# An attention, expert and feed-forward kernel: its first sixteen attention groups and first sixteen product pieces in one written order of stages, with another order of loads

## The chip, the cores and the metric

The kernel runs on one core of a Trainium2 chip. A core has five engines that run side by side, each through its own queue in program order: TensorE (PE; PEld is its weight load), VectorE (DVE), ScalarE (ACT), GpSimd (POOL) and SyncE (SP), which here only issues transfers. They wait for one another through semaphores. The metric is device time in microseconds (us) of one execution, the median of several runs; less is better.

## The reference

Three layers follow one another, all in float32: a masked attention, a dense mixture of 8 experts with a gate that is balanced by eight rounds of row and column scaling, and a feed-forward layer. Cut to what matters:

```python
# q, k, v: (4 batches, 8 heads, 576, 64); heads 0-3 local, heads 4-7 strided
scores = scale * np.matmul(q, k.transpose(0, 1, 3, 2))
mask_local = (rel >= 0) & (rel < 32)
mask_strided = (rel >= 0) & (pos[None, :] % 32 == pos[:, None] % 32)
...
attn = softmax(np.where(masks, scores, -1e9))
x = np.matmul(attn, v)             # becomes 2304 tokens x 512
...
P = balanced(np.exp(x @ w_gate))   # 2304 x 8
for e in range(8):
    out += P[:, e:e + 1] * (np.maximum(x @ w1[e], 0.0) @ w2[e])   # 512 -> 1024 -> 512
...
h = out @ w_in                     # 512 -> 2048
result = (h * sigmoid(1.702 * h)) @ w_out
```

## The kernel before

**Products.** Every float32 matrix product is done with each factor split into a high and a low part of a type that TensorE takes in one pass (fp32r): high by an ACT copy, low by a subtraction on DVE or POOL, and three of the four part products are summed. For weights this is `split_into` (ACT L270, POOL or DVE L264), for inputs `split_input` (ACT L576, DVE or POOL L581). Experts are worked off in units of 256 hidden columns over a block of 768 tokens. Work on units is cut into **pieces**, numbered in one list from 0 on: a product of six matmuls (L1048), or a "down" piece, the second product of one tile of 128 tokens (L1314 to L1316, six matmuls). `advance()` issues the next piece and with it the tasks in `side[number]` (splits, sums, loads). The first two units are done plainly, in halves of 384 tokens (`half_product`): pieces 0 to 3 are four products of unit 0, from piece 4 on products and downs alternate. Each second product of a column is followed by `activate`: high part on ACT (hh, L1085), low part on DVE (hl, L1088); a down piece needs the hh and hl of the half before it.

**Attention.** There are 32 attention groups. A local group (two tiles of 96 queries, two heads) goes through score matmuls S (PE L770), mask M (DVE L785), row maximum L (DVE L795), exponential E (ACT L802, four), reciprocal of the sums D (DVE L814, L815), scaling N (POOL L816), transposition T (PE L827), copy out C (ACT or DVE), value product V (PE L851) and copy K into the block of tokens (DVE L863). A strided, "compact" group has the same stages with other instructions (S is L665, C is four ACT copies L723, T runs on DVE). X below is `split_input` of a quarter of the block, W and Y are `split_plain` and `split_w2`, splits of the first two units' weights.

**What sets the order.** A step i issues N and D of group i-2, V and K of group i-4, T and C of i-3, E of i-1, then S, M and L of group i: lockstep, one new group each step. Between the stages stand gaps. In steps 0 to 9 a gap gives idle matmuls that read only zeros (`keep_warm`, L1461), 1.5 on average; in steps 10 to 15 it gives 0.6 pieces and otherwise an idle matmul; from step 16 on it gives 1.5 pieces:

```python
for i in range(NSTEP):
    if i == NHALF + 4:
        quota[0] = 0.0
    att_step(i, fill_first if i < NHALF + 4 else fill_half if i < NFIRST + 4 else fill)
    for t in ahead.pop(i, ()):
        t()
```

`ahead` holds, by step, the weight loads and the splits W, Y and X. Before the first step the loads are issued on SP's queue: the two first local pairs, their values, two compact pairs, their values. When the last step is over, pieces go on until piece 105 is done; then the gate and all else follow in a fixed order.

Of the kernel before, what the change touches and what calls it, by code (L numbers as in the profile page):

```python
# [8 lines left out]
F32 = mybir.dt.float32  # L9
# [3 lines left out]
ALU = mybir.AluOpType  # L13
# [18 lines left out]
IDLE_FIRST = 6  # L32
IDLE_GAP = 1.5


RATE_HALF = 0.6
# [21 lines left out]
def strided_attention_moe_ffn(  # L58
# [643 lines left out]
    def compact_normalise(i, b, pair):  # L702
        _, s, st = att[b, pair, -1]
        den = st[:, 1, :]
        nc.vector.tensor_reduce(out=den, in_=s, axis=AX.X, op=ALU.add)
        nc.vector.tensor_scalar_add(den, den, EPS)
        nc.vector.reciprocal(out=den, in_=den)
        nc.gpsimd.tensor_tensor(
            out=s, in0=s, in1=den[:, :, None].to_broadcast([P, 2 * CQ, CLEN]), op=ALU.mult
        )  # L710

    def compact_transpose(i, b, pair):
        e, _, _ = att[b, pair, -1]
        eT = ap.tile([P, 4, P], F32, tag="eT", name="eT")
        nc.vector.transpose(eT.rearrange("p n q -> p (n q)"), e)
        src = eT.rearrange("p n (m q) -> p (n m) q", q=Q)
        for c in range(CG):
            rows = slice(c * Q, c * Q + CLEN)
            o = wide[rows, :, c * CLEN : (c + 1) * CLEN]
            if c % 2 and i >= NFIRST:  # L720
                nc.gpsimd.tensor_copy(o, src[rows, :, :CLEN])
            else:
                nc.scalar.activation(out=o, in_=src[rows, :, :CLEN], func=AF.Copy)  # L723

    def compact_values(i, b, pair):
# [3 lines left out]
        for h in range(2):  # L729
            if i < NALONE:  # L730
                av = ps.tile([P, 512], F32, tag="AB"[h], name="av")
            elif h:
                av = down_bank("av") if i >= NFIRST else ps.tile([P, 512], F32, tag="B", name="av")
            else:
                av = eps.tile([P, 512], F32, tag="pa", name="av")
# [74 lines left out]
    def att_normalise(i, b, pair, g):  # L810
        s, st, U, R, C = att[b, pair, g]
        n = 2 * U
        den = st[:R, 1, :n]
        nc.vector.tensor_scalar_add(den, den, EPS)  # L814
        nc.vector.reciprocal(out=den, in_=den)  # L815
        nc.gpsimd.tensor_tensor(  # L816
            out=s, in0=s, in1=den[:, :, None].to_broadcast([R, n, C]), op=ALU.mult
        )

    def att_transpose(i, b, pair, g):  # L820
        s, _, U, R, C = att[b, pair, g]
        if i < NALONE:
            pt = ps.tile([P, 4, P], F32, tag="AB"[i % 2], name="pt")
        else:
            pt = eps.tile([P, 4, P], F32, tag="pa", name="pt")
# [14 lines left out]
    def att_values(i, b, pair, g):  # L840
        eT, U, R, C = att.pop((b, pair, g))
        vt = att_in["v", b, pair]
        if i < NALONE - 1 and i % 2:
            av = ps.tile([P, 512], F32, tag="C", name="av")
        elif NALONE - 1 <= i < NFIRST:
            av = ps.tile([P, 512], F32, tag="B", name="av")
        else:
            av = down_bank("av")
# [36 lines left out]
    NALONE = NHALF + 1  # L885
    STAGES = [
        (2, att_normalise, False),
        (4, att_values, True),
        (3, att_transpose, True),
        (1, att_exp, False),  # L890
        (0, att_scores, True),
    ]
# [14 lines left out]
    def att_step(i, fill):  # L907
# [11 lines left out]
        def loads():  # L919
            for p in LOAD_QK[i]:  # L920
                load_qk(*p, q=nc.scalar)
            for p in LOAD_V[i]:
                load_v(*p, q=nc.scalar)

        if i < NHALF + 4:
            for d, stage, gap in STAGES:
                for t in run(d, stage):
                    t()
                if gap:
                    fill()  # L930
        else:
            run(2, att_normalise)
            first, apart = run(4, att_values), 4 <= i < n + 4 and groups[i - 4][2] < 0
            if apart:
                for t in first:
                    t()
                first = ()
                fill()
            second, third = run(3, att_transpose), run(0, att_scores)
            for t in first + second:  # L940
                t()
            if not apart:
                fill()
            for t in third[:1]:
                t()
            run(1, att_exp)
            loads()
            fill()
            for t in third[1:]:
                t()  # L950
            fill()
        if i < NHALF + 4:
            loads()

# [498 lines left out]
    with tc.manual_schedule():  # L1453
# [39 lines left out]

        quota = [0.0]
        ahead = defaultdict(list)
        QUARTERS = ("W11", "W21", "W12", "W22")
        ahead[1].append(lambda: load_w1(0))
        ahead[3].append(lambda: load_w2(0))
        ahead[4].append(lambda: load_w1(1))
        for m, pair in enumerate(PAIRS[:2]):  # L1500
            ahead[5 + m].append(lambda pair=pair: load_vc(1, pair))
        for n, what in enumerate(QUARTERS):
            ahead[(4, 5, 7, 8)[n]].append(lambda what=what: split_plain(0, what))
            ahead[9 + n].append(lambda what=what: split_plain(1, what))
        for ft in range(2):
            ahead[7 + ft].append(lambda ft=ft: split_w2(0, ft))
            ahead[12 + ft].append(lambda ft=ft: split_w2(1, ft))
        ahead[10].append(lambda: load_w1(2))
        ahead[9].append(lambda: load_w2(1))

        ahead[NHALF + 2].append(lambda: split_input(0))
        ahead[NHALF + 3].append(lambda: split_input(3))
        ahead[14].append(lambda: split_input(6))
        ahead[NFIRST + 3].append(lambda: split_input("X21"))
        BY_HALF = 4 * PLAIN + 3 * (PLAIN - 1)

        def fill_first():
            quota[0] += IDLE_GAP
            keep_warm(int(quota[0]))
            quota[0] -= int(quota[0])  # L1520

        def fill_half():
            quota[0] += RATE_HALF
            if quota[0] >= 1 and done[0] < BY_HALF:
                advance()
                quota[0] -= 1
            else:
                keep_warm(1)
# [7 lines left out]
        plan_first_sums()  # L1536
        side[20].append(lambda: gate_logits(0))
        for i in range(NSTEP):
            if i == NHALF + 4:
                quota[0] = 0.0  # L1540
            att_step(i, fill_first if i < NHALF + 4 else fill_half if i < NFIRST + 4 else fill)
            for t in ahead.pop(i, ()):
                t()
# [115 lines left out]
```

## Time and profile before

| | us |
|---|---|
| median of 3 runs (1958.81 to 1960.32) | 1959.04 |
| the profiled execution, its own time | 1957.69 |
| its span, first to last instruction | 1955.9 |
| PE busy in the span | 1917.5 (98%) |
| DVE busy | 1455.9 (74%) |
| ACT busy | 853.1 (44%) |
| POOL busy | 1244.9 (64%) |

A time is read against the engines: where PE is busy all the time, only less work for PE helps; where it isn't, the order of the work and its waits set the time. PE's busy time counts idle matmuls too. In rows, "us" after a start is a duration; "[1.2 <-DVE e L785]" says that the engine stood idle for 1.2 us before, until that instruction of DVE was done.

### The profile page before, as it was taken

How to read it: one execution, taken by the hardware profiler on the slowest of the kernel's cores; microseconds unless marked ns; L12 is line 12 of the kernel's file. 1: busy time of each engine (PE TensorE's matmuls, PEld its weight loads, DVE VectorE, ACT ScalarE, POOL GpSimd, SP SyncE). 2: the span in 40 equal slices, each digit the busy share in tenths (PEclk: the TensorE clock that was granted, in tenths of full speed). 3: DMA queues.
4: the chain of work that ended last, by engine and by line, in shares of the span. 5: the costliest groups of instructions: out<-in, count | busy, mean ns of one | idle time of the engine just before them, and what ended most of it. 6: DMA issues, size and time to landing. Idle time of an engine off the chain costs nothing.

```text
span 1955.9 us, 35146 instructions
## 1 busy us (share of the span) xinstructions
PE 1917.5 (98%) x11716; PEld 1792.3 (92%) x11716; DVE 1455.9 (74%) x2715; ACT 853.1 (44%) x2079; POOL 1244.9 (64%) x1282
## 2 busy tenths in 40 slices
PE   7999999999999999999999999999999999999999
PEld 5778778888888999999999999999999998888888
DVE  5788677777677788788878788888886766756555
ACT  4555456666765433333333433333333445533332
POOL 3456566777777677777767888888887767600100
PEclk8999999999999999999999999999999999999999
DMA  6468789999997998988898789999999867665663
GB/s 219 149 217 289 263 283 325 368 344 354 367 330 246 317 311 288 299 288 287 282 297 288 252 302 313 333 321 323 358 312 325 288 220 266 233 193 186 218 196 122
DMA packets 284451, 546.18 MB, mean 279 GB/s; under 512 B 30864, under 2 KB 52720, under 8 KB 283376
## 3 DMA queue, kind: packets, MB, share of 16 engines
q1 hardware_dynamic: 280816, 532.08, 79.4%
q10 hardware_dynamic: 3456, 11.87, 2.0%
q8 instruction: 94, 1.54, 0.3%
q14 instruction: 85, 0.70, 0.1%
HBM read 382.30 MB, written 161.53 MB: 278 GB/s over the span
## 4 chain that ended last, share of the span: by engine, by line
PE 62%; DVE 2%; DMA 2%; POOL 2%; issue 1%; ACT 0%; SPq 0%; ACTq 0%; DVEq 0%; POOLq 0%
PE y L1209 21%; PE pA L1048 17%; PE pC L1048 9%; PE pB L1048 4%; PE y L1316 4%; PE y L1315 4%; PE y L1314 4%; DMA w<-s1moe 1%; POOL s L1181 1%; DMA w<-s7moe 1%; POOL comb L1156 1%; DMA rows<-prd 0%; DVE xs L565 0%; DMA ws<-fw 0%; DVE r L1162 0%
## 5 line engine op out<-in xcount | busy, mean ns | idle before, releaser
L1048 PE MATMUL pA<-xc,w 128*128 128x384 f32 x2880 | 573.4, 336 | 2.7 <-DVE pB L1104 2.2
L1209 PE MATMUL y<-comb,w 128*128 128x384 f32 x2688 | 537.8, 334 | 2.2 <-DVE sum L1219 1.0
L1048 PEld LDWEIGHTS pA<-xc,w 128*128 128x128 f32 x2880 | 508.9, 188 | 19.8 <-DVE pB L1104 3.6
L1209 PEld LDWEIGHTS y<-comb,w 128*128 128x128 f32 x2688 | 472.0, 188 | 3.5 <-DVE sum L1219 1.7
L1156 POOL TENSOR_TENSOR comb<-s,comb 128x384 fp32r<-128x384 f32 x256 | 283.5, 1118 | 91.4 <-ACT comb L1151 82.3
L1219 DVE TENSOR_TENSOR sum<-y,sum 128x384 f32<-128x384 f32 x420 | 231.4, 552 | 100.2 <-PE y L1209 97.7
L1048 PE MATMUL pC<-xc,w 128*128 128x384 f32 x1464 | 295.8, 336 | 0.0
L1316 PE MATMUL y<-w,hl 128*128 128x512 f32 x672 | 268.3, 399 | 5.0 <-DVE hl L1088 4.6
L1314 PE MATMUL y<-w,hh 128*128 128x512 f32 x672 | 264.3, 393 | 6.8 <-DVE acc L1329 2.8
L1048 PEld LDWEIGHTS pC<-xc,w 128*128 128x128 f32 x1464 | 259.8, 188 | 9.8
L1315 PE MATMUL y<-w,hh 128*128 128x512 f32 x672 | 265.6, 395 | 0.0
L1151 ACT ACTIVATE comb<-r 128x384 fp32r<-128x384 f32 x192 | 101.3, 528 | 363.1 <-DVE r L1162 350.0
L1316 PEld LDWEIGHTS y<-w,hl 128*128 128x128 f32 x672 | 126.2, 188 | 36.0 <-DVE hl L1088 8.8
L1314 PEld LDWEIGHTS y<-w,hh 128*128 128x128 f32 x672 | 126.4, 188 | 27.0 <-DVE acc L1329 3.4
L264 POOL TENSOR_TENSOR w<-raw,w 128x512 fp32r<-128x512 f32 (+1 forms) x104 | 120.8, 1176 | 35.7 <-ACT w L270 35.4
L1048 PE MATMUL pB<-xc,w 128*128 128x384 f32 x708 | 142.2, 335 | 0.0
L1315 PEld LDWEIGHTS y<-w,hh 128*128 128x128 f32 x672 | 126.2, 188 | 15.8
L1156 POOL TENSOR_TENSOR comb<-r,comb 128x384 fp32r<-128x384 f32 x64 | 67.8, 1060 | 112.7 <-ACT comb L1151 112.7
L270 ACT ACTIVATE w<-raw 128x256 fp32r<-128x256 f32 (+1 forms) x307 | 135.6, 461 | 8.9 <-POOL raw L234 8.8
L1151 ACT ACTIVATE comb<-s 128x384 fp32r<-128x384 f32 x256 | 131.8, 515 | 11.0 <-POOL s L1181 10.9
L1181 POOL TENSOR_TENSOR s<-r,r 128x384 f32<-128x384 f32 x127 | 134.2, 1077 | 2.1 <-DVE r L1162 2.0
L1343 DVE TENSOR_TENSOR acc<-y,acc 128x512 f32<-128x512 f32 x126 | 86.8, 689 | 62.7 <-PE y L1316 62.6
(178 smaller groups left out, 2827.2 us busy)
## 6 DMA issues: line engine op xcount, KB each, us to landing
w<-s1moe SPq DMA_DIRECT2D x448, 256.0 KB, 4.9
w<-s7moe SPq DMA_DIRECT2D x448, 256.0 KB, 4.9
s1moe<-w SPq DMA_DIRECT2D x216, 256.0 KB, 5.0
w<-s1ffn SPq DMA_DIRECT2D x133, 256.0 KB, 2.8
s7moe<-kw SPq DMA_DIRECT2D x116, 256.0 KB, 4.9
s7moe<-w SPq DMA_DIRECT2D x96, 256.0 KB, 4.8
w<-s2ffn SPq DMA_DIRECT2D x38, 512.0 KB, 3.7
raw<-wa SPq DMA_DIRECT2D x32, 512.0 KB, 5.9
```

Of the source, the lines that this page charges most:

```text
L264: eng.tensor_tensor(out=t[:, 1], in0=src, in1=f(high), op=ALU.subtract)
L270: nc.scalar.activation(out=high, in_=src, func=AF.Copy)
L1048: nc.tensor.matmul(out=o, lhsT=w[:, hw, kk * P : (kk + 1) * P], rhs=x[:, hx, kk, :], start=opens and m == 0, stop=ends and m == len(todo) - 1,
L1151: nc.scalar.activation(out=t[:, 0, :], in_=part[i, q], func=AF.Copy)
L1156: eng.tensor_tensor(out=t[:, 1, :], in0=part[i, q], in1=f(t[:, 0, :]), op=ALU.subtract)
L1181: eng.tensor_tensor(out=part[i, q], in0=part[i, a], in1=part[i, b], op=op)
L1209: nc.tensor.matmul(out=o, lhsT=t[:, hw, dt * P : (dt + 1) * P], rhs=x[:, hx, :], start=(n == 0), stop=(n == 5))
L1219: nc.vector.tensor_tensor(out=a, in0=o, in1=a, op=ALU.add)
L1314: nc.tensor.matmul(out=o, lhsT=hh[:, c], rhs=w[:, 0], start=(m == 0), stop=False)
L1315: nc.tensor.matmul(out=o, lhsT=hh[:, c], rhs=w[:, 1], start=False, stop=False)
L1316: nc.tensor.matmul(out=o, lhsT=hl[:, c], rhs=w[:, 0], start=False, stop=(m == 1))
L1343: nc.vector.tensor_tensor(out=a, in0=y, in1=a, op=ALU.add)
```

## The change

The sixteen first steps are replaced by a list of tokens, START, worked off in order. A letter is a stage and the number its group: S scores, M mask, L maximum, E exponential, D sums and reciprocal, N scaling, T transposition, C its copy, V values, K copy into the block. `:p`, `:A`, `:B`, `:C` name the PSUM bank. i3 is three idle matmuls, W, Y and X are the splits, q and v loads of a pair, A2 and B1 weight loads, P the next piece. So stages that went together (M and L with S, N with D, C with T, K with V) are issued apart. After START the steps 16 to 35 run as before, and the same piece, 105, is reached where they end. START holds pieces 0 to 15; sixteen steps held 0 to 9.

```diff
+START = (
+    "S0 M0 i2 S1 L0 M1 E0 L1 i2 S2 E1 D0 N0 M2 q12 L2 i3 T0:p D1 S4 E2 N1 C0 M4 V0:B L4 T1:p D2 S3 E4 M3 "
+    "N2 C1 L3 i3 V1:C D4 E3 T2 N4 K1 i2 S8 K0 C2 T4:p D3 M8 N3 i1 S6 L8 C4 T3:A M6 E8 V4:B C3 V3:C K4 D8 "
+    "W210 S5 W110 K3 W120 L6 X0 V2:BC E6 K2 P0 q13 N8 D6 M5 N6 T8:p L5 S7 C8 E5 V8:B D5 T6:p q10 M7 N5 C6 "
+    "K8 L7 W121 i1 V6:B W221 T5 E7 S9 v10 D7 v11 C5 K6 N7 M9 Y00 T7 i3 V5:BC W111 L9 W220 S10 q11 Y01 K5 "
+    "E9 M10 X3 i2 S12 W211 A2 C7 D9 i1 P1 B1 L10 N9 V7:pB M12 E10 T9 P2 K7 C9 P3 D10 L12 N10 S11 P4 E12 "
+    "M11 L11 P5 Y11 Y10 V9:pB E11 K9 P6 D11 T10:p D12 N11 X6 P7 N12 C10 T11:p S13 V10:B q22 C11 P8 K10 "
+    "M13 V11:B K11 P9 XX21 T12:p S14 P10 L13 C12 P11 E13 M14 P12 S15 q20 D13 i1 P13 L14 N13 M15 E14 L15 "
+    "P14 i3 P15 "
+).split()
...
         nc.scalar.dma_start(out=cst, in_=consts)
+        load_qk(0, PAIRS[0])
         for p in EARLY:
             load_qk(*p, rest)
             load_v(*p)
-        for pair in PAIRS[:2]:
-            load_qk(0, pair)
-        for pair in PAIRS[:2]:
-            load_vc(0, pair)
+        load_vc(0, PAIRS[0])
+        load_qk(0, PAIRS[1])
+        load_vc(0, PAIRS[1])
         nc.gpsimd.memset(wide, 0.0)
         nc.vector.memset(wgr, 0.0)
+        load_w1(0)
         nc.sync.dma_start(out=wgr[:, :, :E], in_=wg)
+        load_w2(0)
+        load_w1(1)
+        for pair in PAIRS[:2]:
+            load_vc(1, pair)
...
+        for token in START:
+            key, _, banks = token.partition(":")
+            if key[0] == "i":
+                keep_warm(int(key[1:]))
+            elif key[0] == "P":
+                advance()
+            else:
+                ops[key](tuple(BANK[x] for x in banks))
         quota = [0.0]
```

SP's queue, the first loads, before (a row is one transfer or several alike; qkt are queries and keys, vt and vc values; qkt_133 is the first compact pair):

```order
L638 DMA qkt_116<-qk 128x2x192 x2
L638 DMA qkt_116<-qk 128x2x384
L648 DMA vt_128<-vw 128x768
L638 DMA qkt_116<-qk 128x2x384
L648 DMA vt_131<-vw 128x768
L641 DMA qkt_133<-qk 128x1152
L641 DMA qkt_135<-qk 128x1152
L655 DMA vc_137<-vc 128x1024
L655 DMA vc_139<-vc 128x1024
L1478 DMA wgr_88<-wg 128x4x8
L217 DMA raw1_175<-wa 128x1024
```

and of the change, where the first compact pair is qkt_127:

```order
L646 DMA qkt_116<-qk 128x2x192 x2
L649 DMA qkt_127<-qk 128x1152
L646 DMA qkt_116<-qk 128x2x384
L656 DMA vt_130<-vw 128x768
L646 DMA qkt_116<-qk 128x2x384
L656 DMA vt_133<-vw 128x768
L663 DMA vc_135<-vc 128x1024
L649 DMA qkt_137<-qk 128x1152
L663 DMA vc_139<-vc 128x1024
L225 DMA raw1_143<-wa 128x1024
L1498 DMA wgr_88<-wg 128x4x8
```

That pair's load moves ahead of four transfers, and the first weight load (raw1) stands behind the compact values as before, now ahead of the gate's.

PE's queue around the first piece (pA is its output, xc the split input, w1 a split weight, sc scores, av values, pt a transposition), before:

```order
L827 MATMUL pt_660<-cst_87,e_470 128x96 x4
L1461 MATMUL idle_out_115<-idle_113 128x384
L665 MATMUL sc_672<-qkt_575 32x18 x64
L1461 MATMUL idle_out_115<-idle_113 128x384 x2
L851 MATMUL av_759<-eT_665,vt_128 64x96 x4
L770 MATMUL sc_770<-qkt_613 96x128 x4
L1461 MATMUL idle_out_115<-idle_113 128x384
L1048 MATMUL pA_781<-xc_625,w1_323 128x384 x6
L1461 MATMUL idle_out_115<-idle_113 128x384
L739 MATMUL av_800<-wide_110,vc_425 64x72 x8
L739 MATMUL av_809<-wide_110,vc_425 64x72 x8
L1048 MATMUL pA_781<-xc_624,w1_427 128x384 x6
```

and of the change:

```order
L857 MATMUL av_376<-eT_350,vt_133 64x96 x4
L857 MATMUL av_382<-eT_370,vt_130 64x96 x4
L673 MATMUL sc_394<-qkt_137 32x18 x64
L752 MATMUL av_481<-wide_110,vc_135 64x72 x8
L752 MATMUL av_490<-wide_110,vc_135 64x72 x8
L1067 MATMUL pA_505<-xc_472,w1_462 128x384 x6
L838 MATMUL pt_520<-cst_87,e_338 128x96 x4
L673 MATMUL sc_528<-qkt_257 32x18 x64
L857 MATMUL av_598<-eT_525,vt_133 64x96 x4
L838 MATMUL pt_606<-cst_87,e_361 128x96 x4
L1480 MATMUL idle_out_115<-idle_113 128x384
L857 MATMUL av_625<-eT_611,vt_130 64x96 x4
```

The first product stands between the values of the first compact group and a transposition, more than twenty rows earlier on PE, with one idle matmul near it in place of five.

ACT's queue around the first two high parts (hh11 and hh12), before:

```order
L723 ACTIVATE wide_110<-eT_764 18x16x18 x4
L700 ACTIVATE e_737<-e_737 128x16x18
L270 ACTIVATE w1_790<-raw1_321 128x256
L1085 ACTIVATE hh11_828<-pA_781 128x384
L802 ACTIVATE e_775,st_776<-e_775,st_776 96x128 x4
L648 DMA vt_851<-vw 128x768
L270 ACTIVATE w1_862<-raw1_321 128x256
L723 ACTIVATE wide_110<-eT_873 18x16x18 x4
L1085 ACTIVATE hh12_893<-pC_855 128x384
```

and of the change:

```order
L708 ACTIVATE e_702<-e_702 128x16x18
L584 ACTIVATE xc_471<-x_103 128x768
L278 ACTIVATE w1_786<-raw1_148 128x256
L736 ACTIVATE wide_110<-eT_724 18x16x18 x4
L1104 ACTIVATE hh11_806<-pA_505 128x384
L815 ACTIVATE e_762,st_763<-e_762,st_763 96x128 x4
L736 ACTIVATE wide_110<-eT_837 18x16x18 x4
L1104 ACTIVATE hh12_860<-pC_839 128x384
```

Before, the four copies into `wide` stood straight ahead of the second high part alone, and a weight split ahead of the first; now they stand straight ahead of both, and the next exponentials (e) behind.

## Rows read from the trace of the kernel before

**Rows 1.** Busy time of each engine in four stretches of the span

```profile
core 0: us, PE busy (x) PEld busy (x) DVE busy (x) ACT busy (x) POOL busy (x), PEclk, DMA share, GB/s
0.00:78.83 78.83, 63.12 (x955) 49.77 (x956) 46.08 (x111) 38.56 (x132) 27.22 (x35) 0.85 0.60 199
78.83:100.00 21.17, 20.87 (x280) 17.36 (x281) 15.78 (x32) 10.28 (x32) 13.48 (x15) 1.00 0.38 124
100.00:200.00 100.00, 96.48 (x1054) 80.35 (x1053) 81.51 (x175) 54.91 (x179) 60.03 (x72) 1.00 0.76 261
200.00:300.00 100.00, 92.81 (x519) 78.94 (x519) 71.78 (x163) 50.58 (x139) 64.81 (x81) 0.98 0.79 272
```

**Rows 2.** By line, first 78.83 us: count, busy us, mean ns, idle before

```profile
L1461 PE MATMUL idle_out<-idle 128*128 128x384 f32 x59 | 22.6, 472 | 1.3 <-DVE idle L1456 1.3
L802 ACT ACTIVATE e<-e,st 96x128 f32<-96x128 f32 x44 | 17.2, 392 | 8.2 <-DVE st L795 8.1
...
L785 DVE SCALAR_TENSOR_TENSOR e<-sc,msk 96x512 f32<-96x512 f32 x12 | 8.2, 682 | 8.4 <-PE sc L770 8.1
...
L581 DVE TENSOR_TENSOR xc<-x,xc 128x768 fp32r<-128x768 f32 x3 | 3.5, 1155 | 2.4 <-ACT xc L576 2.4
...
L814 DVE TENSOR_SCALAR st<-st 96x4 f32<-96x4 f32 x10 | 2.9, 287 | 1.2 <-ACT e L802 1.2
...
L1327 DVE COPY acc<-y 128x512 f32<-128x512 f32 x3 | 2.1, 692 | 2.6 <-PE y L1316 2.6
...
L1088 DVE SCALAR_TENSOR_TENSOR hl<-pA,hh 128x384 fp32r<-128x384 f32 x2 | 1.1, 553 | 1.1 <-ACT hh L1085 1.1
```

**Rows 3.** In order of time, 5 to 52 us: start, duration, engine, line

```profile
5.72 0.69 DVE L785 SCALAR_TENSOR_TENSOR e<-sc,msk 96x512 f32<-96x512 f32 x1 [4.31 <-PE sc L770]
...
12.56 1.40 PE L665 MATMUL sc<-qkt 64*32 64x18 f32 x128 [3.89 <-DMA qkt<-qk]
...
15.48 0.16 DVE L814 TENSOR_SCALAR st<-st 96x4 f32<-96x4 f32 x1
...
28.59 1.17 PE L770 MATMUL sc<-qkt 64*96 64x128 f32 x8
...
35.94 1.48 POOL L264 TENSOR_TENSOR w<-raw,w 128x512 fp32r<-128x512 f32 x1
...
36.22 1.23 DVE L814 TENSOR_SCALAR st<-st 96x4 f32<-96x4 f32 x1
...
51.63 2.12 PE L1048 MATMUL pA<-xc,w 128*128 128x384 f32 x6
```

**Rows 4.** In order of time, 78 to 90 us: the same columns

```profile
78.83 0.55 PE L851 MATMUL av<-eT,vt 128*64 128x96 f32 x8
...
80.99 1.31 PE L1048 MATMUL pC<-xc,w 128*128 128x384 f32 x6
...
83.21 0.74 POOL L264 TENSOR_TENSOR w<-raw,w 128x256 fp32r<-128x256 f32 x1 [0.47 <-ACT w L270]
...
85.37 1.25 DVE L565 TENSOR_TENSOR S<-x 128x768 f32<-128x768 f32 x1
...
87.09 0.55 PE L851 MATMUL av<-eT,vt 128*64 128x96 f32 x8
...
87.58 1.83 POOL L581 TENSOR_TENSOR xc<-S,xc 128x768 fp32r<-128x768 f32 x1 [1.77 <-ACT xc L576]
...
88.05 0.68 PE L770 MATMUL sc<-qkt 64*96 64x128 f32 x8
...
88.66 1.33 PE L1048 MATMUL pC<-xc,w 128*128 128x384 f32 x6
...
89.83 0.39 PE L1314 MATMUL y<-w,hh 128*128 128x512 f32 x1
```

**Rows 5.** TensorE: stretch, length, busy, granted clock, DMA share, GB/s

```profile
28.00:32.00 4.00, 4.00 (x22) 0.50 0.55 194
```

More of the change, by code (lines that the diff above doesn't have):

```diff
@@ L716, in compact_transpose, with copy, named_bank, compact_values @@
         src = eT.rearrange("p n (m q) -> p (n m) q", q=Q)
[L717 to L725, printed above, removed]
+        def copy():
+            for c in range(CG):
+                rows = slice(c * Q, c * Q + CLEN)
+                o = wide[rows, :, c * CLEN : (c + 1) * CLEN]
+                if c % 2 and i >= NFIRST:
+                    nc.gpsimd.tensor_copy(o, src[rows, :, :CLEN])
+                else:
+                    nc.scalar.activation(out=o, in_=src[rows, :, :CLEN], func=AF.Copy)
+        return (copy,)
+    def named_bank(tag, name):
+        return (eps if tag == "pa" else ps).tile([P, 512], F32, tag=tag, name=name)
+    def compact_values(i, b, pair, banks=None):
         vt = att_in["v", b, pair]
@@ L729, in compact_values @@
         for h in range(2):
[L730 to L735, printed above, removed]
+            av = named_bank(banks[h], "av") if banks else (down_bank("av") if h else named_bank("pa", "av"))
             for m in range(CQ // 2):
@@ L838, in att_transpose, with att_values @@
         return (copy,)
-    def att_values(i, b, pair, g):
+    def att_values(i, b, pair, g, banks=None):
         eT, U, R, C = att.pop((b, pair, g))
         vt = att_in["v", b, pair]
[L843 to L848, printed above, removed]
+        av = named_bank(banks[0], "av") if banks else down_bank("av")
         for u in range(U):
@@ L917, in run @@
             return stage(i - d, b, pair, g) or ()
-        def loads():
+        for t in run(2, att_normalise):
+            t()
+        first, apart = run(4, att_values), 4 <= i < n + 4 and groups[i - 4][2] < 0
+        if apart:
+            for t in first:
+                t()
+            first = ()
+            fill()
+        second, third = run(3, att_transpose), run(0, att_scores)
+        for t in first + second:
+            t()
+        if not apart:
+            fill()
+        for t in third[:1]:
+            t()
@@ L920, in loads @@
             for p in LOAD_QK[i]:
-                load_qk(*p, q=nc.scalar)
+                ops[f"q{p[0]}{p[1]}"] = lambda _, p=p: load_qk(*p, q=nc.scalar)
             for p in LOAD_V[i]:
[L923 to L951, printed above, removed]
@@ L952, in att_step @@
-        if i < NHALF + 4:
-            loads()
+                ops[f"v{p[0]}{p[1]}"] = lambda _, p=p: load_v(*p, q=nc.scalar)
     def gate_logits(blk):
@@ L1492, in advance @@
             done[0] += 1
-        quota = [0.0]
[L1495 to L1528, printed above, removed]
+        ops = {}
+        start_ops(ops)
+        for u in range(PLAIN):
+            for what in ("W11", "W21", "W12", "W22"):
+                ops[f"{what}{u}"] = lambda _, u=u, what=what: split_plain(u, what)
+            for ft in range(2):
+                ops[f"Y{u}{ft}"] = lambda _, u=u, ft=ft: split_w2(u, ft)
+        ops["B1"] = lambda _: load_w2(1)
+        ops["A2"] = lambda _: load_w1(2)
+        for m in (0, 3, 6, "X21"):
+            ops[f"X{m}"] = lambda _, m=m: split_input(m)
+        plan_first_sums()
+        side[20].append(lambda: gate_logits(0))
+        for token in START:
[4 more added lines that the diff above has]
+                advance()
+            else:
+                ops[key](tuple(BANK[x] for x in banks))
+        quota = [0.0]
         def fill():
@@ L1534, in fill @@
                 quota[0] -= 1
[L1536 to L1543, printed above, removed]
+        for i in range(NLIST, NSTEP):
+            att_step(i, fill)
         while done[0] // PPU % 2 or done[0] % PPU < 2:
```

62 lines of the change are left out of this document (41 added, 21 removed).

## The prediction

> **What bounds the kernel now.** I read the busy times by stretch first, since a share over 1956 us says nothing of its first 4%. From 78.83 us on PE is busy 20.87 of 21.17 us, then 96.48 of 100, then 92.81 of 100, at a granted clock of 0.98 to 1.00 [rows 1]: behind that point more or less product work is what costs. Before it PE counts 63.12 of 78.83 us, but the groups by line show that 22.6 us of these are the 59 idle matmuls [rows 2]. Some 40.5 us do work, and DVE is next with 46.08 us [rows 1]. So no engine fills the start: the lockstep sets it. The waits by line tell the same: DVE's masks alone waited 8.4 us for scores, and the low parts of the inputs 2.4 us for ACT [rows 2]. The order of time gives single gaps: PE stood 3.89 us until the first compact pair had landed at 12.56, and the first product ran only at 51.63 [rows 3].
>
> At 78.83 PE takes the values of group 12, the first work of step 16 [rows 4]. By then pieces 0 to 9 are issued. The changed kernel comes to the same place with pieces 0 to 15. So the question is when it gets there, against 78.83 us plus the price of six pieces.
>
> **The six pieces.** Before, piece 10 starts at 80.99, and pieces 10 to 14 run without other PE work until 87.09: 6.10 us. Piece 15 runs from 88.66 to 89.83: 1.17 us [rows 4]. Together 7.27, and the comparable time is 78.83 + 7.27 = 86.1 us.
>
> **What the start must hold.** DVE does its 46.08 us [rows 1], and within START also what stood behind 78.83: one low part of an input (about 0.95, the shortest of a group with mean 1.155), one of an hh (0.553), two additions of down pieces (2 x 0.692) [rows 2], one input sum (1.25) [rows 4], and one row maximum that took as long as a mask (0.68) [rows 2]. That is 4.8, so 50.9 us. POOL gets 27.22 [rows 1] plus three weight quarters (3 x 0.74), one low part (1.83) [rows 4] and four subtractions of a quarter's size (estimated at 0.74 each): 34.2 us. PE's work is 40.5 + 7.3 = 48 us beside 27 idle matmuls, 10 us at the mean of 0.38 between the two clocks' prices. DVE stays the fullest, and its queue is what I follow.
>
> **The walk along DVE's queue.** I went through START with each stage at its duration in the trace (exponentials 4 x 0.392 us, about 1.65 with the last read [rows 2]), each engine in its own order, each stage when its input is there. The first mask is at 5.72 as before [rows 3]; nothing ahead of it moves. From there DVE has work except for these waits:
> - the first groups, with little else to do: 0.5 for the second scores, 1.15 for the compact scores, 0.35 for the fourth group: 2.0. The compact pair lies behind half as many bytes as before, and its scores come at about 9 in place of 12.56, as soon as the score banks are free;
> - exponentials that end just ahead of their reciprocal (groups 8 and 11): 2.25;
> - ACT's high part ahead of an input's low part (three of four): 1.75;
> - the hh of the first two products, each behind four copies into wide (some 1.8 us, order of ACT above): 0.9 and 1.8, so 2.7. Piece 5 is late with them;
> - the y of two down pieces: 1.85.
>
> These are 10.5 us. Their sum: 5.7 + 50.4 (without the two clears ahead of the first mask) + 10.5 = 66.6 us. PE runs out of pieces at the same time: by the walk, the first product starts at 25.7, the second at 38.6 (input of the second compact pair), piece 5 at 46.3, and piece 15 is over at about 67 to 68.
>
> **Two surcharges.** First, small DVE work is stretched where POOL works. A reciprocal's first instruction takes 0.16 us at 15.48, and 1.23 at 36.22, while POOL's 1.48 us split lies over it [rows 3]. Ten such instructions and three low parts took 2.9 and 3.5 us [rows 2], against 10 x 0.16 and 3 x 0.95: 1.95 us in 13. Some 8 others of their kind at the same mean make it 3.2, which the 46.08 hold. POOL's share rises from 27.2/78.8 to about 34/70, and there are some 24 of them, so 3.2 x 1.4 x 24/21 = 5.1: 2 us more. The Trainium skill ("SBUF — State Buffer", section "SBUF: two separate sides") calls the port pair of the two engines an exclusive lock, which the later one waits out in full. The trace agrees with it for the reciprocal, 1.23 against 0.16, and not for masks, which read PSUM, 0.682 on average; locked throughout, the two engines' work would lie end to end, rival 3.
>
> Second, the clock. In a stretch with granted clock 0.50 the scores take 1.17 us [rows 3, 5], at full clock 0.68 [rows 1, 4]. I have walked with a mix. With 27 idle matmuls in place of 59, I take five more handoffs at half clock, 0.5 each: 2.5 us. Both ends: none (66.6), or the case of rival 2.
>
> So START reaches group 12's values at 66.6 + 2 + 2.5 = 71.1 us, against 86.1: 15.0 us gained. Behind it the order of pieces and steps is the same, with 4.5 pieces a step; pieces merely stand six further on against the groups. There PE idles 0.3 and 3.5 us up to 200 us [rows 1]; I allow 1 us for new meetings of DVE's work. **Sum: 14.0 us.** The profiled execution took 1957.69 us on its own clock, 1.35 below the median 1959.04; so 1943.7 in its terms, 1945.0 in the median's.
>
> **Costed at nothing:** the two early W and Y loads stand behind the compact values on SP; the walk needs the first weights only at 22.6 us. Were they late, product 0 alone would be, and piece 1 waits until 38.6 anyhow: up to 13 us of cover. Loads on ACT's queue stand behind stages that free their buffer; that of group 13's pair (q22) holds ACT until scores 13 are read, which the walk has done by 55 with ACT at 54. If it were late, the last input's split and the last high part are behind it.
>
> **Rivals.**
> 1. The waits hide the surcharges. Everything in the walk holds, and stretches fall into DVE's 10.5 us of waits. START ends at 65 to 68, gain 17.5 to 21: 1938 to 1941.5. For it: exponentials and copies do lie beside stretches. Against it: before, neither hid everything.
> 2. PE's clock falls in START. Products at half clock take 2.12 us [rows 3], against 1.04 to 1.17 above. If fourteen more stages on the path run at 0.50, at 0.5 us each, 7 us of the 14 are gone: gain 4 to 10, 1949 to 1955. For it: between 28 and 32 us the clock was 0.50 although PE was busy 4.00 of 4.00 us [rows 5]. The Trainium skill ("TensorE: Matmul & The Clock Gate", Part 1) says that idleness throttles the clock to 1.2 GHz and sustained work frees it. By that rule fewer idle matmuls mean more time at 0.50; no trace of before has so few, and by it the time would be 1949 to 1955.
> 3. The end on the other side: DVE and POOL shut each other out. End to end they make 5.7 + (50.4 - 3.2) + 34.2 = 87.1 us; with the waits of DVE that neither covers, the first 2.0 and the 1.85 for PE, 91.0, so 4.9 us slower than 86.1: 1964. It decides from stretches of some 20 us on (71.1 - 5.1 + 20 = 86), where 3.2 stand now, 12% of POOL's time; it would need some 60%. The masks and the copies out of PSUM, unstretched, speak against it.
> 4. The written order meets the same waits under other names (bank or buffer held, a load behind a store on SP), and START ends at 82 to 90: no change, 1955 to 1963. Against it: in the walk each ring buffer was free by at least 0.5 us.
>
> **Chances.** The forecast (gain 10 to 17.5) 0.56; rival 1 0.13; rival 2 0.17; rival 4, within 0.2% (3.9 us, about what a measurement can tell), 0.08; slower, rival 3 in the main, 0.06. Faster is 0.56 + 0.13 + 0.17 = 0.86. From a gain of 20 down to one of 5.5 the range is 1939 to 1953.5: it leaves out the edge of rival 1, the lower part of rival 2, and rivals 3 and 4, together 0.2.
>
> **What would show it.** In the profile after: PE takes group 12's values at about 71 (68 to 76); first product near 26, second near 39; compact scores at about 9; idle matmuls 27, near 8 to 12 us. Rival 1 shows as 65 to 68 there; rival 2 as a mean clock below 0.75 up to that point; rival 3 as many 0.15 us instructions of DVE at over 1 us. Wrong altogether, if that point comes at 71 and the end moves by less than 8: then PE idles more between 70 and 300 us.

## The result and the profile after

The changed kernel takes 1942.24 us, the median of 4 runs (1940.33 to 1943.53); beside it the kernel before took 1958.92 (1956.92 to 1960.32). The ratio is 0.9915, with a 95% interval of 0.9898 to 0.9932. The forecast was 1945.0, with a range from 1939 to 1953.5. The profiled execution took 1940.98 us, with a span of 1939.2.

The prediction's mark, where PE takes group 12's values behind piece 15, comes at 69.34 us. PE in order of time (start, duration, engine, line), around the stages that the walk gave times for:

```profile
6.62 1.17 PE L783 MATMUL sc<-qkt 64*96 64x128 f32 x8 [0.46 <-DMA qkt<-qk]
...
9.16 1.45 PE L673 MATMUL sc<-qkt 64*32 64x18 f32 x128 [0.44 <-DMA qkt<-qk]
...
14.27 0.68 PE L783 MATMUL sc<-qkt 64*96 64x128 f32 x8
...
22.64 1.07 PE L673 MATMUL sc<-qkt 64*32 64x18 f32 x104
24.98 0.32 PE L673 MATMUL sc<-qkt 64*32 64x18 f32 x24 [1.28 <-issue]
25.23 1.22 PE L752 MATMUL av<-wide,vc 128*64 128x72 f32 x32
26.38 1.31 PE L1067 MATMUL pA<-xc,w 128*128 128x384 f32 x6
...
39.31 0.34 PE L1067 MATMUL pA<-xc,w 128*128 128x384 f32 x1
40.21 1.15 PE L1067 MATMUL pA<-xc,w 128*128 128x384 f32 x5 [0.56 <-DVE xc L589]
...
68.21 1.21 PE L1067 MATMUL pC<-xc,w 128*128 128x384 f32 x6
69.34 0.55 PE L857 MATMUL av<-eT,vt 128*64 128x96 f32 x8
```

The compact scores start at 9.16, the first product at 26.38 and the second at 39.31. The local scores at 6.62 take 1.17 us and those at 14.27 take 0.68, so PE is at its lower level (1.2 GHz) at first and at its higher one (2.4 GHz) from about 12 us on. At 24.98 PE pauses 1.28 us in the middle of one group of scores. The view names no releaser, only "issue".

The busy times by stretch answer to [rows 1] (the same columns). At the mark the comparable time of before is 86.1, so 86.1 - 69.34 = 16.8 us are won:

```profile
0.00:69.34 69.34, 57.40 (x962) 45.24 (x962) 51.51 (x118) 40.73 (x138) 31.22 (x37) 1.00 0.67 236
...
100.00:200.00 100.00, 93.73 (x1001) 77.80 (x998) 76.28 (x170) 52.96 (x172) 61.87 (x77) 0.97 0.75 259
```

DVE is busy 51.51 of 69.34 us where it was 46.08 of 78.83, and the clock column gives 1.00 in place of 0.85, although PE was at its lower level for the first 12 us. From 100 to 200 us PE is busy 93.73 where it was 96.48: a part seems to be given back. How much, one row shows: the first reduction of the gate, which runs when piece 105 is done. It stood at 244.28 in the kernel before, and stands at 230.08 now (VectorE in order of time):

```profile
230.08 0.29 DVE L993 TENSOR_REDUCE sk<-pr 128x1 f32<-128x144 f32 x1
```

14.2 us are left of 16.8. The span is 16.7 shorter (1955.9 to 1939.2). The last 2.5 us come behind the gate, in code that the change doesn't touch. In the fourteen profiles of this document that stretch takes between 1707.9 and 1711.8 us (the span less the time of this row), so 2.5 us there are no more than executions differ by.

What VectorE waited for from 5 to 70 us (engine, line, releaser: total us, times, longest):

```profile
DVE e L798 <- PE sc L783: 6.0, 3, 3.9
DVE st L827 <- ACT e L815: 2.7, 3, 1.6
DVE hl L1107 <- ACT hh L1104: 2.2, 2, 1.9
DVE acc L1346 <- PE y L1335: 1.2, 1, 1.2
DVE e L689 <- POOL e L830: 1.2, 1, 1.2
DVE acc L1348 <- PE y L1335: 0.8, 1, 0.8
DVE xc L589 <- ACT xc L584: 0.7, 2, 0.4
```

By line, the first 67 us of VectorE's two stretched groups and TensorE's idle matmuls (count, busy us, mean ns, idle before) answer to [rows 2]; three more idle matmuls stand at 67.68, so 30 come ahead of the mark:

```profile
L1480 PE MATMUL idle_out<-idle 128*128 128x384 f32 x27 | 10.2, 480 | 1.3 <-DVE idle L1475 1.3
...
L589 DVE TENSOR_TENSOR xc<-x,xc 128x768 fp32r<-128x768 f32 x4 | 5.5, 1377 | 0.8 <-ACT xc L584 0.7
...
L827 DVE TENSOR_SCALAR st<-st 96x4 f32<-96x4 f32 x10 | 2.6, 259 | 2.7 <-ACT e L815 2.7
```

### The profile page after: what moved, and what is told of

It is laid out like the page before. It is cut to its first block, busy times and chain, and to the rows that moved or that the text cites. A ratio compares the mean times of both kernels' runs of the same rounds, so it can differ in the third digit from the quotient of the medians.

```text
span 1939.2 us, 35075 instructions
## 1 busy us (share of the span) xinstructions
PE 1907.1 (98%) x11687; PEld 1783.2 (92%) x11687; DVE 1454.4 (75%) x2715; ACT 851.8 (44%) x2079; POOL 1244.9 (64%) x1282
## 4 chain that ended last, share of the span: by engine, by line
PE 65%; DVE 2%; POOL 1%; DMA 1%; issue 0%; ACT 0%; SPq 0%; ACTq 0%; DVEq 0%
PE y L1228 22%; PE pA L1067 18%; PE pC L1067 9%; PE pB L1067 5%; PE y L1335 4%; PE y L1334 4%; PE y L1333 4%; DMA w<-s7moe 1%; DMA w<-s1moe 0%; POOL s L1200 0%; POOL comb L1175 0%; DVE comb L1175 0%; POOL xc L589 0%; DVE xc L593 0%; DVE r L1181 0%
## 5 line engine op out<-in xcount | busy, mean ns | idle before, releaser
L1067 PEld LDWEIGHTS pC<-xc,w 128*128 128x128 f32 x1464 | 258.9, 188 | 10.5 <-issue 0.9
```

The costliest lines, as they stand in the source:

```text
L1067: nc.tensor.matmul(out=o, lhsT=w[:, hw, kk * P : (kk + 1) * P], rhs=x[:, hx, kk, :], start=opens and m == 0, stop=ends and m == len(todo) - 1,
```

## The experiments

The theory: the written order lets each engine start a stage when its input is there, DVE's queue sets when START ends, the new order of loads is worth the part of the first groups' waits, and the idle matmuls keep PE's clock. Rivals: the loads alone do it; PE's clock or its supply of instructions holds START, not DVE; it matters how many pieces the start holds.

Below, **mark** is the start of group 12's values, **gate** that of the reduction above. They are 78.83 and 244.28 in the kernel before (its mark is 86.1 with six more pieces), 69.34 and 230.08 in the changed one. The first four kernels ran on one chip, where the kernel before took 1955.51; the next four on another, where it took 1956.38; each ran once. The last four were timed in five rounds, on the first chip again. A mark comes from one profile, which is one execution, and two executions of the changed kernel differ by 3.8 us at the mark; so a mark is compared with the execution in which PE ran most alike.

**The order of loads, undone and alone.** The first kernel is the changed one with the loads as before; the second is the kernel before with the new loads, the same edit the other way round.

```diff
-        load_qk(0, PAIRS[0])
         for p in EARLY:
             load_qk(*p, rest)
             load_v(*p)
-        load_vc(0, PAIRS[0])
-        load_qk(0, PAIRS[1])
-        load_vc(0, PAIRS[1])
+        for pair in PAIRS[:2]:
+            load_qk(0, pair)
+        for pair in PAIRS[:2]:
+            load_vc(0, pair)
```

> The changed kernel with the loads ahead of the first scores in their old order; START is untouched. The mark to read is the time at which PE takes group 12's values (78.83 us before, 69.34 after, there with six pieces more, worth 7.27). Theory: early on DVE has too little other work to cover a late compact pair, and its queue keeps order, so the compact scores come at about 12.5 in place of 9.16 and the mark moves by most of it, to 72 to 73. Rival: DVE's 10 us of later waits take it up, and the mark stays within 1 us of 69.3.

> The kernel before with only the first loads in the new order, lockstep untouched. Theory: the compact scores come some 3.5 us sooner, the mark falls from 78.83 to about 75.5, and so the loads are a fifth of the gain of 16.8 at the mark and the order of stages the rest. Rival: in lockstep nothing behind them is ready sooner, and the mark stays within 1 us of 78.8; then loads and order only pay together.

Measured: with the old loads 1950.52, mark 76.99, gate 237.82. With the new loads alone 1953.85, mark 73.59, gate 242.3. TensorE's compact scores in the two kernels, in this order:

```profile
12.31 1.45 PE L673 MATMUL sc<-qkt 64*32 64x18 f32 x128 [3.72 <-DMA qkt<-qk]
8.34 1.44 PE L665 MATMUL sc<-qkt 64*32 64x18 f32 x128
```

With the old loads the mark is 7.65 later than in the changed kernel's first execution, but not all of it is the loads': PE was at its lower level until about 32 us here and until 12 there. In the changed kernel's second execution (shown under "Timed together") it was so until about 28. Beside that one the compact scores are 3.84 later (12.31 against 8.47) and the mark 3.82 (76.99 against 73.17): the delay goes through in full. In the lockstep the compact scores come 4.2 sooner (12.56 to 8.34) and the mark 5.2 (78.83 to 73.59). The time of that one run is 1.7 below the run beside it (1955.51) and 3.3 below the median of eleven later runs of the kernel before on this chip (1957.10), which differ among themselves by 3.6. So at the mark the loads pay 3.8 to 5.2 us under either order; that they pay less in the lockstep's time isn't shown. What the second kernel did from 20 to 50 us (busy time by stretch):

```profile
20.00:30.00 10.00, 8.28 (x99) 6.14 (x99) 5.32 (x15) 3.42 (x13) 3.89 (x6) 0.65 0.64 219
...
40.00:50.00 10.00, 7.65 (x160) 6.24 (x159) 7.18 (x17) 5.17 (x16) 2.97 (x4) 0.67 0.59 193
```

DVE is busy 5.32 to 7.18 of 10 us: the lockstep leaves it idle, wherever the data are. The granted clock is 0.65 to 0.67, although all 59 idle matmuls are there.

**The idle matmuls, left out and doubled.** The third kernel is the changed one with no idle matmul issued in START (24 fewer ahead of the mark; the six at the very start stay). The fourth is the kernel before with twice as many per gap.

```diff
             if key[0] == "i":
-                keep_warm(int(key[1:]))
+                pass
```
```diff
-IDLE_GAP = 1.5
+IDLE_GAP = 3.0
```

> The changed kernel without the 21 idle matmuls in START (the six at the very start stay). Theory, from the result: the granted clock stayed at 1.00 because of real work, so the clock stays there, and the mark moves by less than 1.5 us, rather down. Rival: the idle matmuls hold the clock up; without them it falls below 0.9 in stretches from 10 to 60 us, scores take 1.17 us, and the mark rises to 72 to 76.

> The kernel before with 3 idle matmuls for each gap of the first ten steps in place of 1.5 (90 in place of 45). Theory: the order of stages holds the start of before, not PE's clock, so the clock rises from 0.80 to over 0.9 between 10 and 60 us and the mark moves by less than 2 us either way. Rival: half-clock stretches made the start of before long; with the clock up the mark falls by 3 us or more.

Measured: without them 1950.87, mark 72.10, gate 239.0; doubled 1954.3, mark 76.58, gate 244.5. The kernel without them, busy time by stretch, and one row of PE:

```profile
36.00:44.00 8.00, 7.21 (x66) 5.84 (x66) 4.83 (x10) 5.14 (x12) 6.16 (x6) 0.50 0.96 355
...
134.50:138.50 4.00, 0.10 (x11) 0.00 (x0) 0.00 (x0) 0.00 (x0) 0.00 (x0) 0.73 1.03 394
...
138.50 0.30 PE L673 MATMUL sc<-qkt 64*32 64x18 f32 x5 [3.91 <-issue]
```

The one run without the idle matmuls took 7 to 9 us more than the changed kernel's medians (1942.24, and 1943.89 further below). Nothing of that stands at the mark, which lies between the changed kernel's two executions (69.34 and 73.17). It comes between mark and gate, 166.9 us in place of 160.7, and 3.9 of these 6.2 are one pause: PE stops in the middle of a group of scores until 138.50, and from 134.5 to 138.5 no other engine works either. In the changed kernel's two profiles the longest pause there without a releaser is 0.5 us. So what the idle matmuls are worth isn't shown by this run; another kernel below took from 1942.89 to 1951.35 in five. In the kernel before, more of them bring 2.25 us at the mark and 1.2 in the time, with one run each; runs of the kernel before differ by up to 3.6, and the changed kernel's two marks by 3.8. The Trainium skill ("TensorE: Matmul & The Clock Gate", Part 1) says that idleness throttles the clock. The 0.50 from 36 to 44 us agrees with it where the changed kernel's first execution has 1.00; but the second execution, with its idle matmuls, has 0.61 from 36 to 40.

**Ten pieces in place of sixteen.** The fifth kernel has P10 to P15 taken out of START.

```diff
-    ... "P8 K10 M13 V11:B K11 P9 XX21 T12:p S14 P10 L13 C12 P11 E13 M14 P12 S15 q20 D13 i1 P13 L14 ... P14 i3 P15"
+    ... "P8 K10 M13 V11:B K11 P9 XX21 T12:p S14 L13 C12 E13 M14 S15 q20 D13 i1 L14 ... i3"
```

> The changed kernel with pieces 10 to 15 (and no others) taken out of START; they follow in the later steps, as before. Theory: pieces at the end of START cost their PE time and no more, so the mark comes 7.3 us or a little less sooner, at 62 to 64, and the whole time stays within 3 us of the changed kernel: the gain is not in having sixteen pieces. Rival: the six pieces filled gaps that otherwise stay, the mark comes only 3 to 5 us sooner, and the end is 2 to 5 us later.

Measured: 1945.83, mark 68.82 (76.1 with the six pieces' 7.27), gate 235.2. Without its last six pieces START ends 0.5 us sooner than in the changed kernel's first execution and 4.4 sooner than in its second, not 7.27: a part of that work fits beside the chain of the last groups. So 2.9 to 6.8 us at the mark (76.1 less 73.17 or 69.34) come from filling START with pieces, and the gate is 1.1 to 5.1 later. This run doesn't narrow that down: its clock was 0.88 from 10 to 60 us, and two PE pauses named "issue" took 1.30 and 2.77 us.

**Two orders meant to be better.** The walk blames 2.7 us on high parts behind the wide copies, 2.25 on late exponentials. The sixth kernel takes piece 3 ahead of the copies C9; the seventh does so too, and takes the exponentials and scaling of group 11 ahead of the splits Y11 and Y10.

```diff
-    "... P2 K7 C9 P3 D10 ..."
+    "... P2 K7 P3 C9 D10 ..."
-    "M11 L11 P5 Y11 Y10 V9:pB E11 K9 P6 D11 T10:p D12 N11 X6 P7 ..."
+    "M11 L11 P5 E11 V9:pB K9 P6 D11 T10:p N11 D12 Y11 Y10 X6 P7 ..."
```

> The changed kernel with piece 3 ahead of the four copies of group 9, so that ACT makes its high part first. In the changed kernel DVE waited 1.92 us for it at 47.03. Theory (DVE's queue sets START): that wait goes, all behind it comes 1.0 to 1.5 us sooner, and the mark falls to 68 or 68.5. Rival: piece 5 and what follows on PE has no time to give, and the wait comes back at the next input: mark unchanged within 0.4.

> As the run with the high part first, and group 11's exponential and scaling moved ahead of the second unit's two w2 splits on ACT and POOL. In the changed kernel PE stood 1.95 us until group 11 was scaled. Theory: that wait goes too, mark at 66.5 to 67.5. Rival: the splits come too late for piece 12, or the wait moves behind, and the mark is not below that of the run with the high part first alone.

Measured: 1947.35, mark 70.57, gate 233.7; and 1945.56, mark 74.00, gate 234.1. Neither time is below the changed kernel's, and neither mark is below its first. But both executions were late before they came to the edit: PE was at its lower level until about 28 us. In the sixth kernel (TensorE, then VectorE's wait for high parts from 5 to 70 us):

```profile
42.17 0.34 PE L1067 MATMUL pA<-xc,w 128*128 128x384 f32 x1
...
70.57 0.55 PE L857 MATMUL av<-eT,vt 128*64 128x96 f32 x8
...
DVE hl L1107 <- ACT hh L1104: 1.1, 2, 0.9
```

The wait of 1.9 us went (1.1 in two waits, the longest 0.9). From the second product, the last milestone ahead of the edit, to the mark it took 28.4 us (42.17 to 70.57), where the changed kernel took 30.0 (39.31 to 69.34) and 31.3 (41.88 to 73.17). So this part of START is some 1.6 us shorter, about what the theory says, though the time of the one run doesn't show it. In the seventh the same stretch took 29.95 us (44.05 to 74.00), with the clock at 0.64 from 40 to 50 us; nothing of its further edit can be seen.

**Work taken from DVE.** The eighth kernel is the changed one without the row maxima of the twelve local groups in START. Twelve instructions of 0.673 us, 8.1 us, leave DVE's queue; the exponentials take zero as their bias.

```diff
-        return mask, largest
+        return (mask, lambda: None) if i < NLIST else (mask, largest)
...
-                bias=st[:R, 0, n : n + 1],
+                bias=zero[:R] if i < NLIST else st[:R, 0, n : n + 1],
```

> The changed kernel without the row maximum of the first sixteen groups' local ones (the exponential takes a bias of zero): 12 instructions of DVE at 0.67 us, 8.1 us, are left out, with the same output up to rounding as long as no score is large. Theory: DVE's queue sets START, so the mark falls by 4 to 7 us, to 62 to 65, and the rest is taken up by waits for ACT and PE. Rival: ACT, POOL or PE would hold it as well; the mark falls by less than 2 us.

Measured: 1943.14, mark 70.40, gate 231.5. The mark is 1.1 later than in the changed kernel's first execution and 2.8 sooner than in its second. VectorE's waits from 5 to 70 us in that kernel:

```profile
DVE e L799 <- PE sc L784: 8.8, 4, 4.0
DVE hl L1108 <- ACT hh L1105: 4.7, 3, 2.3
DVE x L879 <- PE av L753: 1.9, 2, 1.4
DVE acc L1347 <- PE y L1336: 1.7, 2, 1.2
DVE acc L1349 <- PE y L1336: 1.5, 2, 0.8
```

Against the changed kernel's, scores go from 6.0 to 8.8, hh from 2.2 to 4.7, the compact values from under 0.3 to 1.9 and the downs from 2.0 to 3.2: 8.1 us of work became some 8 us of waiting, nearly all for PE or for ACT behind PE. PE in order of time says why:

```profile
21.50 1.07 PE L674 MATMUL sc<-qkt 64*32 64x18 f32 x104
24.45 0.41 PE L674 MATMUL sc<-qkt 64*32 64x18 f32 x24 [1.88 <-issue]
24.79 2.19 PE L753 MATMUL av<-wide,vc 128*64 128x72 f32 x32
26.91 2.29 PE L1068 MATMUL pA<-xc,w 128*128 128x384 f32 x6
...
37.01 0.46 PE L784 MATMUL sc<-qkt 64*96 64x128 f32 x3
39.98 0.56 PE L784 MATMUL sc<-qkt 64*96 64x128 f32 x5 [2.51 <-issue]
```

Two pauses in the middle of a group take 4.4 us, and the compact values and the product last 2.19 and 2.29 us where the changed kernel's last 1.22 and 1.31: PE is at its lower level (1.2 GHz). So in this execution PE took back much of what DVE was given, and the mark doesn't tell alone what the 8.1 us are worth. From the second product to the mark, where six of the twelve maxima were, it took 27.5 us (42.91 to 70.40) in place of the changed kernel's 30.0.

**Timed together.** The last four kernels ask what is left of each reading in medians: the changed kernel again; the changed kernel with 14 more idle matmuls where PE waits; the changed kernel with the old loads; and one with all that was meant to be better (no maxima, piece 3 and group 11's exponentials first, the 14 idle matmuls).

```diff
-    ... C1 L3 i3 V1:C ... D3 M8 N3 i1 S6 ... Y00 T7 i3 V5:BC ... C7 D9 i1 P1 ... N12 C10 T11:p ...
+    ... C1 L3 i5 V1:C ... D3 M8 N3 i2 S6 ... Y00 T7 i8 V5:BC ... C7 D9 i3 P1 ... N12 C10 i4 T11:p ...
```

> The changed kernel once more, nothing edited, beside the next three on one chip. Its first profile had TensorE at full speed from 12.5 us on, and the mark (PE takes group 12's values) at 69.34; the one-look runs so far, with nearly the same order, were at half speed up to 10 to 31 us and again near 40. Theory: this differs from execution to execution and is worth little, mark 69 to 73, time 1940 to 1944 where before is near 1957 to 1959. Rival: full speed belongs to this order, and the mark comes again within 0.5 of 69.3.

> The changed kernel with 14 more idle matmuls, put where PE waited anyway (ahead of the values of groups 1 and 5, ahead of the scores of group 6, piece 1 and the transposition of group 11). Theory: they keep the clock up between 33 and 47 us where one-look runs fell to half speed, cost nothing, and the time is 1 to 2 us below the changed kernel's on the same chip. Rival: the clock has no price in START, because DVE and ACT hold it; the time is the same within 0.5 or above it by the idle matmuls, up to 3.

> The old load order in the changed kernel again, now timed on one chip with it. The one look gave a mark of 76.99, 7.65 later, where 2.5 to 3.4 were expected. Theory: the compact scores come 3.4 later and all behind them with them, and the rest of the 7.65 was TensorE's clock in that execution; the time is 3 to 4 us above the changed kernel's. Rival: the order of stages leans on the new loads, more than the first wait is lost, and the time is 6 to 8 us above.

> All at once: no row maximum in the first sixteen groups' local ones (8.1 us of DVE work left out), piece 3's high part ahead of group 9's copies, group 11's exponential ahead of the w2 splits, and the idle matmuls in waits. Theory (DVE's queue sets START, the clock took the gain of the one-look run): mark at 62 to 66 and the time 3 to 7 us below the changed kernel's. Rival: TensorE and its supply of instructions hold START as much as DVE, and the time is within 2 us of it.

| kernel | median us (lowest to highest) | ratio to before, 95% | mark | gate |
|---|---|---|---|---|
| before (11 runs) | 1957.10 (1955.73 to 1959.29) | | | |
| changed, again | 1943.89 (1938.63 to 1945.56) | 0.9929, 0.9917 to 0.9941 | 73.17 | 234.06 |
| 14 more idle matmuls | 1946.64 (1942.89 to 1951.35) | 0.9950, 0.9937 to 0.9962 | 70.08 | 234.02 |
| old loads | 1949.46 (1947.31 to 1953.84) | 0.9963, 0.9951 to 0.9975 | 77.33 | 238.33 |
| all together (6 runs) | 1941.97 (1936.35 to 1944.69) | 0.9915, 0.9901 to 0.9928 | 68.77 | 230.38 |

The loads: 1949.46 - 1943.89 = 5.6 us, and the intervals don't touch. With the old ones the compact scores of the written order start at 12.98, as they did at 12.56 in the kernel before [rows 3], not at 9 (TensorE, kernel with the old loads):

```profile
12.98 1.46 PE L673 MATMUL sc<-qkt 64*32 64x18 f32 x128 [4.59 <-DMA qkt<-qk]
```

So of this chip's 13.2 us the written order has 7.6 (1957.10 - 1949.46), and the loads 5.6 when they stand under it. At the mark 4.2 of these stand (77.33 against 73.17), about the 4.5 by which the compact scores are later (12.98 against 8.47 below).

The same program again has its mark at 73.17, not 69.34. TensorE in order of time in the second execution:

```profile
8.47 1.47 PE L673 MATMUL sc<-qkt 64*32 64x18 f32 x128
...
14.54 1.17 PE L783 MATMUL sc<-qkt 64*96 64x128 f32 x8
...
24.68 1.47 PE L673 MATMUL sc<-qkt 64*32 64x18 f32 x128
26.08 1.49 PE L752 MATMUL av<-wide,vc 128*64 128x72 f32 x32
27.49 1.69 PE L1067 MATMUL pA<-xc,w 128*128 128x384 f32 x6
...
41.88 0.34 PE L1067 MATMUL pA<-xc,w 128*128 128x384 f32 x1
...
73.17 0.55 PE L857 MATMUL av<-eT,vt 128*64 128x96 f32 x8
```

The local scores at 14.54 take 1.17 us, in the first execution 0.68 at 14.27. Half speed lasts here until about 28 us, and nothing of the order is different. The first product is 1.1 us later (27.49 against 26.38), the mark 3.8, after two more stretches with a lower clock (0.61 from 36 to 40 us, 0.72 from 56 to 62).

With 14 more idle matmuls the clock column gives 1.00 through START (busy time by stretch, where the changed kernel's second execution has 0.85 and 0.87):

```profile
30.00:40.00 10.00, 7.52 (x208) 6.03 (x208) 8.44 (x22) 6.59 (x16) 6.01 (x8) 1.00 0.74 231
...
50.00:60.00 10.00, 8.36 (x61) 6.57 (x60) 7.30 (x17) 5.64 (x20) 5.27 (x4) 1.00 0.39 139
```

The changed kernel's first execution had 1.00 without them, and the last kernel, which has them, 0.84 from 30 to 40 us; so they aren't shown to hold the clock. The mark is 3.1 sooner than the changed kernel's in that round, but the gate comes at the same time, and the median is 2.7 later, with intervals that overlap (up to 0.9941, from 0.9937). A sooner mark isn't a sooner end. The last kernel is 1.9 below the changed one, with intervals that overlap widely, as its rival said: no better version is shown. But its nearest neighbour is the kernel with 14 more idle matmuls, from which it differs only in the work and the waits taken from DVE. Beside that one it is 4.7 us faster (1941.97 against 1946.64), and the intervals don't touch (up to 0.9928, from 0.9937); the mark is 1.3 sooner, the gate 3.6. So relieving DVE does pay, though by less than the 8.1 us of work that are gone.

## Why the prediction was right

**The sum.** The forecast gain of 14.0 us compares with 16.7 in the first comparison and 13.2 in the second. Its milestones, which the walk gave without the two surcharges, hold to within 1.6 us: compact scores 9 (measured 9.16), first product 25.7 (26.38), second 38.6 (39.31, and 40.21 for all but its first matmul), piece 15 over by 67 to 68 (68.21 + 1.21 = 69.4); piece 5, the first down, is at 46.51 where 46.3 was forecast. The mark of 71.1 lies between two executions of the same program, 69.34 and 73.17. So the walk was as good as one execution can tell. The kernel with the old loads confirms its first step in reverse: compact scores at 12.98.

Term by term the first execution has 5.26 us to the first mask (5.7 forecast), 51.0 of DVE's work from there (50.4 and 2 of stretch), 10.9 in the waits below (10.5), and 2.2 in shorter waits and gaps that no term held; the 2.5 for the clock don't show as a term of their own. Two misses of over 2 us stand against each other there, so a part of the nearness is luck.

**The waits of DVE.** Forecast 10.5 us, measured 10.9. From the waits view: first groups 3.3 (scores 6.0 less the 3.9 ahead of the first mask, plus 1.2 for POOL's e) against 2.0, exponentials 2.7 against 2.25 (groups 8 and 11, which the walk named, 0.66 and 1.59), hh 2.2 against 2.7, y 2.0 against 1.85. ACT's high parts cost 0.7 against 1.75. DVE's work up to the mark was 51.5 where 50.9 was forecast and 2 us of stretch on top.

**The stretch.** The reciprocals' first instruction takes 259 ns on average and the low parts 1377. Worked as the prediction did, 10 x (259 - 160) + 4 x (1377 - 950) = 2.7 us in 14 instructions, so 4.6 in 24: 1.4 us more than 3.2, where 2 were allowed. Rival 3 wanted some 20; it falls. The Trainium skill's rule ("SBUF — State Buffer", section "SBUF: two separate sides"), by which the later of DVE and POOL waits the lock out, agrees with the trace row by row. Of the ten, eight have no POOL work beside them and take 0.13 to 0.17 us. The other two take 0.81 and 0.53, and both end within 0.03 us behind the POOL instruction beside them. The first, with POOL's row ahead of it:

```profile
26.63 1.03 POOL L830 TENSOR_TENSOR e<-e,st 96x512 f32<-96x512 f32 x1
26.88 0.81 DVE L827 TENSOR_SCALAR st<-st 96x4 f32<-96x4 f32 x1
```

Masks and row maxima aren't held up: the mask at 48.37 takes 0.68 beside POOL's scaling from 48.02 to 49.06, and the maximum at 42.38 takes 0.67 beside POOL's from 41.95 to 42.62. So the surcharge is small because few of the instructions that can be held up meet POOL's work.

**The clock.** 2.5 us were allowed. What it costs shows between two executions of the same program: PE was at its lower level for about 12 us in the first and for some 35 of 73 in the second (28 at the start, and 7 by the column, an estimate), and the mark is 3.8 later. The prediction counted 27 idle matmuls; 30 come ahead of the mark. Rival 2's "fewer idle matmuls mean more time at 0.50" isn't refuted: the kernel before, with 59, was at its higher level by 6.92 us, where its local scores take 0.68 (TensorE), as were the other two in lockstep by 7 us, while the kernels with START came to it between about 10 and 33 us.

```profile
6.92 0.68 PE L770 MATMUL sc<-qkt 64*96 64x128 f32 x8 [0.17 <-DMA qkt<-qk]
```

What failed in rival 2 is the price: 3.8 us at the mark for 23 us more at the lower level, where rival 2 had 7 for fourteen stages. And 30 idle matmuls gave 12 us in one execution and 35 in another, so how many there are doesn't settle the clock by itself.

**What is given back.** 1.0 us was allowed between the mark and the rest; from mark to gate 2.6 were taken, 160.7 us against 158.2 (165.45 less 7.27). But the two other kernels in lockstep, with the new loads and with doubled idle matmuls, took 161.4 and 160.6 counted the same way. So whether the change gives anything back there isn't shown. With 14 more idle matmuls the stretch took 3.2 us more, for a cause that isn't settled; without idle matmuls 6.2 more, of which 3.9 are the pause shown above.

**The premise that holds only in part: "DVE stays the fullest, and its queue is what I follow".** Following it gave the right times. But DVE doesn't hold START by itself: with 8.1 us less work and the two other orders the mark came 1.3 us sooner beside its nearest neighbour (68.77 against 70.08), and the time 4.7. What DVE is spared becomes waiting for PE, or for ACT behind PE, as in the kernel without maxima, so a chain between them sets the end; PE's speed moved the mark by 3.8 us with DVE's work unchanged. Which share the pauses named "issue" have wasn't tried by itself.

**The loads.** I priced them inside the first groups' waits, 3.56 us from 12.56 to 9. At the mark they are worth 3.8 and 4.2 beside an execution of like PE speed, so the price was about right. The 5.6 in the medians hold about 1.4 more, which comes behind the mark and has no cause shown.

## What to carry to other kernels

A start in which no engine is full can be forecast by walking one engine's queue, with each duration from the trace, to within what two executions of the same program differ by. That the walk lands right doesn't make that engine the bound: take work away from it and see whether the end moves, before the next edit goes there. A mark is to be compared with that of an execution in which PE ran alike: the same old loads looked 7.65 us dear beside one execution of the changed kernel and 3.8 beside another, and only the second agrees with the delay of the first compact scores, 3.84.

## What the runs showed of the hardware

Two things weren't expected. TensorE's matmuls ran at half speed (1.17 us for scores that take 0.68) from the start to about 12 us in one execution of the program and to about 28 in another, while the clock column gives 1.00 for both: there, durations tell the level, and the column doesn't.

And PE paused in the middle of one group of matmuls, waiting for nothing that the profile names: 1.28 us in the changed kernel, 1.30 and 2.77 with ten pieces, 1.88 and 2.51 in the kernel without maxima, 3.91 at 138.50 in the one without idle matmuls. The pauses keep to places in PE's queue and not to times or stages. The first one stands behind the 347th matmul of the program in all three kernels that have it, and in the kernel without idle matmuls, which has 13 fewer ahead of that group and so is further on in it, a pause of 0.30 us stands behind the 347th as well. The second stands behind the 728th in both kernels. The changed kernel's second execution has neither, so the place alone doesn't make a pause. Nor are full DMA engines needed: their share was 1.03 in the pause of 3.91 us and 1.02 in that of 2.51, but 0.15 in the changed kernel's own of 1.28 (its busy times there):

```profile
23.75:24.95 1.20, 0.00 (x0) 0.00 (x0) 0.76 (x2) 1.20 (x3) 1.20 (x3) 1.00 0.15 55
```

That the supply of instructions is late at these places is argued from this, not shown.
